# Output sums held in PSUM banks, and the first product wholly from quarters, in the tail of an attention and mixer kernel

## The chip, the cores and the metric

The kernel runs on one core of a Trainium2 chip. The metric is the device time of one execution in microseconds. Fast executions of one kernel mostly lie within 2 us of each other, and a few lie up to 5 us above, which is more than a small change is worth. So beside the times I use a second measure, from the traces alone: the time **from the V products of batch 5 to the end of the span**. The V products are four matmuls of 512 columns in the token mixing of a batch; those of batch 5 are the last landmark ahead of everything that the change touches.

The measure repeats well. The changed kernel was traced twice, the second time in a slow execution, whose granted clock was low (0.64 and 0.68) only between 10 and 30 us of the span and whose extra time lay entirely ahead of the landmark. Start of the V products in the first trace and in the second, with the spans:

```profile
221.59 0.39 PE L538 MATMUL pscore<-V_sb,ux 32*128 32x512 bf16 x2
core 0: 361.3 us, clock 1.000
```
```profile
227.38 0.39 PE L538 MATMUL pscore<-V_sb,ux 32*128 32x512 bf16 x2
core 0: 367.1 us, clock 0.981
```

361.3 - 221.59 = 139.71 us, and 367.1 - 227.38 = 139.72 us, though the spans differ by 5.8 us. Stretches of equal code agree too: the V products of the last mixing start 75.47 or 75.48 us behind the landmark in the kernel before and in experiments 2, 3 and 6, and 70.76 or 70.77 us behind it in the changed kernel, its repeat and experiments 4, 5, 8, 9 and 11. But the spans are printed to 0.1 us, so the difference of two measures is good to about 0.1 us. Where two kernels have the same end, the start of the last product, printed to 0.01 us, is the sharper mark.

## The reference, cut to what matters

```python
# attention with a decay bias, 8 batches x 8 heads x 576 tokens x 64
scores = scale * q @ k.T;  scores = where(causal, -1e9, scores + minimum(bias, 0))
x = softmax(scores) @ v                      # as (8, 576, 512)
# low-rank token mixing, then the channel mixer
u = x + (x.T @ U @ V).T
out = u + relu(u @ w_ch1) @ w_ch2            # 512 -> 2048 -> 512
```

The mixer's 4608 tokens go in NG = 9 groups of 512. Both mixer products are done by quarters: a 2 x 2 product of blocks with seven block products in place of eight, from sums of blocks, and sums of the seven results.

Of the kernel before, what the change touches and what calls it, by code (L numbers as in the profile page):

```python
# [39 lines left out]
def kernel(  # L40
# [33 lines left out]
    work = ctx.enter_context(tc.tile_pool(name="work", bufs=2))  # L74
    ps_w = ctx.enter_context(tc.tile_pool(name="ps_w", bufs=4, space=bass.MemoryType.PSUM))
    ps_s_pool = tc.tile_pool(name="ps_s", bufs=2, space=bass.MemoryType.PSUM)
# [606 lines left out]
    def outputs_by_quarters(g, hT, u_sd):  # L683
# [3 lines left out]

        def bank():
            return pwork().rearrange("p (i d) -> p i d", i=2)

        def product(acc, a, b, i):
            for kt in range(HF):
                nc.tensor.matmul(  # L693
                    acc[:, i, :],
                    lhsT=a[:, kt, ds(i * 128, 128)],
                    rhs=b[:, kt, :],
                    start=(i == 0 and kt == 0),
                    stop=(kt == HF - 1),
                    skip_group_check=True,
                )  # L700
# [22 lines left out]

        halves = range(2)
        U2 = work.tile([128, 2, HD], FP32, tag="U2", name="U2", bufs=1)
        p1 = bank()
# [43 lines left out]
        send(o22, 1, 1)  # L770
        if g == NG - 1:
            o21 = quarter()
            add_u(o21, U2, 1, 0)
            for i, lo, hi in ((0, 0, HD), (1, 0, 128), (1, 128, HD)):
                p4 = bank()
                for kt in range(HF):
                    nc.tensor.matmul(
                        p4[:, 0, lo:hi],
                        lhsT=A22[:, kt, ds(i * 128, 128)],
                        rhs=B_4[:, kt, lo:hi],  # L780
                        start=(kt == 0),
                        stop=(kt == HF - 1),
                    )
                add(o21[:, i, lo:hi], o21[:, i, lo:hi], p4[:, 0, lo:hi])
                (nc.sync if lo == 128 else nc.scalar).dma_start(
                    out=out_flat[ds(g * 512 + 256 + i * 128, 128), lo:hi], in_=o21[:, i, lo:hi]
                )
            return
        p4 = bank()
# [27 lines left out]
    def first_weight_sums():  # L817
        for dst, a, b, op in (
            (W_3, W11, W21, ALU.subtract),
            (W_1, W21, W22, ALU.add),  # L820
            (W_2, W_1, W11, ALU.subtract),
            (W_4, W12, W_2, ALU.subtract),
        ):
            placed(lambda: nc.vector.tensor_tensor(dst, a, b, op=op))
            yield

# [14 lines left out]
    def hidden_by_quarters(u, u_sums, hT, sets):  # L841
# [36 lines left out]
        def at(e, slot):  # L878
# [29 lines left out]
            elif slot == 13:  # L908
                product(p.w, W22, u_4, e, False)
                add(e, 1, 0, p.U2, p.w)  # L910
                if sets == 4 and e in (1, 2):
                    first_sums(hT, e == 1)
            return True
# [6 lines left out]

    def by_token(u):
        u_sd = work.tile([128, 4, 4, 128], BF16, tag="u_sd", name="u_sd", bufs=1)
        nc.sync.dma_start_transpose(
# [4 lines left out]
    def chanmix(g, hT=None, done=0):  # L928
        u = uT_of.pop(g)
        if g > 0:  # L930
            hT = work.tile([128, NF, 512], BF16, tag="hT", name="hT")
            sums = weight_sums() if g == 1 else iter(())
        for nf in range(done, NF):
# [7 lines left out]
            if nf == (3 if g > 0 else NF - 1):  # L941
                u_sd = by_token(u)
            yield
        if g > 0:
# [23 lines left out]

    fill = []

    pace = [0, 16]

    def step_fill():
        pace[0] += pace[1]
        if pace[0] < 16:
            return
        pace[0] -= 16
        while fill:
            if next(fill[0], fill) is not fill:
                return  # L980
            fill.pop(0)
# [146 lines left out]
    pace[1] = 11  # L1128
    made_w = first_weight_sums()
    for n in range(2 * PB, NP + 2):  # L1130
        b, hp = divmod(n, PB)
        if hp == 0 and b < B - 1:
            load(b + 1)
        if NP - 2 <= n <= NP:
            step(made_w)
        mixing = seqmix(b - 1) if hp == 1 and b > FT else iter(())
# [17 lines left out]
        if hp == 1 and FT < b < B:  # L1154
            fill.append(chanmix(b - 1))
            pace[1] = 12 if b < 4 else 12
        if 2 * PB < n <= NP:
            run(values(n - 1, pT_of(n - 1)))
        if hp == 0 and 2 <= b < B - 1:
            load_v(b + 1)  # L1160
    pace[1] = 16
    ps_s_pool.__exit__(None, None, None)
    ps_t = ctx.enter_context(tc.tile_pool(name="ps_t", bufs=4, space=bass.MemoryType.PSUM))
    tail_sums = {}
    tail_sums[NG - 2] = token_sums(
        uT(NG - 2), v_slots[1].rearrange("p a b c -> p (a b c)")
    )
    step(made_w)
    xT_again = work.tile([128, 4, 640], BF16, tag="xT", name="xT", bufs=1)
# [6 lines left out]

    for g, sets, fills in ((NG - 2, 2, range(13)), (NG - 1, 4, (1, 3, 5, 7, 9, 11, 13, 16, 19, 22, 25, 25, 26, 26))):
        u = uT_of.pop(g)
        hT = work.tile([128, NF, 512], BF16, tag="hT", name="hT")
        if g < NG - 1:  # L1180
            fill.append(hidden_plain(u, hT, (4, 12, 5, 13, 6, 14, 7, 15)))
        for at, _ in enumerate(hidden_by_quarters(u, tail_sums[g], hT, sets)):
# [9 lines left out]
        while fill:  # L1192
            step_fill()
        u_sd = by_token(u)
        fill.append(outputs_by_quarters(g, hT, u_sd))
# [33 lines left out]
```

## The kernel before: what the change and the argument touch

The second product of a group. Each of the seven products takes a fresh bank of four rotating ones. ScalarE and VectorE keep the running sum U2 in SBUF:

```python
U2 = work.tile([128, 2, HD], FP32, tag="U2", bufs=1)
p1 = bank()                                   # pwork(): one of 4 rotating banks
for i in halves: product(p1, A11, B11, i); ...; yield
nc.scalar.copy(U2, p1)
p2 = bank(); ...                              # product(p2, A12, B21)
o = quarter(); add_u(o, U2, 0, 0); add(o, o, p2); send(o, 0, 0)
p6 = bank(); ...; add(U2, U2, p6)
p5 = bank(); ...; o22 = quarter(); add(o22, U2, p5)
p3 = bank(); ...; o12 = quarter(); add_u(o12, o22, 0, 1); add(o12, o12, p3)
p7 = bank(); ...; add_u(o22, o22, 1, 1); add(U2, U2, p7); add(o22, o22, p7)
if g == NG - 1:                               # the end: p4 in three pieces
    o21 = quarter(); add_u(o21, U2, 1, 0)
    for i, lo, hi in ((0, 0, HD), (1, 0, 128), (1, 128, HD)):
        p4 = bank(); ...                      # 8 matmuls
        add(o21[:, i, lo:hi], o21[:, i, lo:hi], p4[:, 0, lo:hi]); ...dma_start(...)
```

`add_u` adds the residual from `u_sd`, the group's tokens turned by a transposing transfer (`by_token`). A `yield` ends a piece; the pieces of a group's mixer are the *fill*, which the loop over the heads runs between its own steps at a pace:

```python
def step_fill():
    pace[0] += pace[1]
    if pace[0] < 16: return
    pace[0] -= 16
    while fill: ...                           # one piece of the first generator
# tail: first product of groups 7 and 8 by quarters, the fill between
for g, sets, fills in ((NG - 2, 2, range(13)), (NG - 1, 4, (1, 3, 5, ...))):
    if g < NG - 1: fill.append(hidden_plain(u, hT, (4, 12, 5, 13, 6, 14, 7, 15)))
    for at, _ in enumerate(hidden_by_quarters(u, tail_sums[g], hT, sets)):
        for _ in range(fills.count(at)): step_fill()
    while fill: step_fill()
    u_sd = by_token(u)
    fill.append(outputs_by_quarters(g, hT, u_sd))
```

The softmax here doesn't subtract the row's maximum and nothing guards it: scores larger than these inputs give would overflow.

## Time and profile before

| | before |
|---|---|
| time, median of 4 runs | 363.95 us (363.54 to 364.96) |
| span of the trace | 362.9 us |
| PE busy, share of the span | 97% |
| V products of batch 5 to the end | 362.9 - 222.30 = 140.60 us |
| start of the last product to the end | 362.9 - 356.69 = 6.21 us |

The lines that carry the reading are in the prediction. Its method is that PE's true pace is read from the spacing of the starts in long runs. A matmul's record is longer than that: 0.273 us against a spacing of 0.109 for 256 columns. These last 0.16 us are pipeline and no work. A wait in brackets is counted from the end of the record before it, so it can be 0.16 us shorter than the hole in the starts. And "x3" in a run of four with a hole of 0.21 us behind it is a record missing from the trace, not a wait.

### The profile page before, as it was taken

How to read it: one execution, taken by the hardware profiler on the slowest of the kernel's cores; microseconds unless marked ns; L12 is line 12 of the kernel's file. 1: busy time of each engine (PE TensorE's matmuls, PEld its weight loads, DVE VectorE, ACT ScalarE, POOL GpSimd, SP SyncE). 2: the span in 40 equal slices, each digit the busy share in tenths (PEclk: the TensorE clock that was granted, in tenths of full speed). 3: DMA queues.
4: the chain of work that ended last, by engine and by line, in shares of the span. 5: the costliest groups of instructions: out<-in, count | busy, mean ns of one | idle time of the engine just before them, and what ended most of it. 6: DMA issues, size and time to landing. Idle time of an engine off the chain costs nothing.

```text
span 362.9 us, 9555 instructions
## 1 busy us (share of the span) xinstructions
PE 351.2 (97%) x3973; PEld 254.9 (70%) x4015; DVE 278.0 (77%) x607; ACT 209.5 (58%) x319; POOL 84.8 (23%) x108
## 2 busy tenths in 40 slices
PE   8899999999999999999999999999999999999995
PEld 4566566666588667876688667876688568678884
DVE  8766776779789758985699569975899279676985
ACT  3784985747762678257843786357734641565710
POOL 8988263614040404040314022000000000000000
PEclk9999999999999999999999999999999999999999
DMA  7999999999999899979994999260213400500053
GB/s 104 170 203 200 162 181 132 155 152 111 118 105 106 149 119 63 94 101 117 133 101 63 141 136 85 52 164 20 20 49 95 89 18 33 144 2 31 29 132 102
DMA packets 155107, 37.94 MB, mean 105 GB/s; under 512 B 138680, under 2 KB 153432, under 8 KB 155064
## 3 DMA queue, kind: packets, MB, share of 16 engines
q0 software_dynamic: 110016, 18.50, 78.9%
q1 hardware_dynamic: 44760, 18.64, 30.0%
q8 instruction: 31, 0.51, 0.7%
q10 hardware_dynamic: 288, 0.20, 0.2%
q14 instruction: 12, 0.10, 0.1%
HBM read 37.25 MB, written 9.70 MB: 129 GB/s over the span
## 4 chain that ended last, share of the span: by engine, by line
PE 77%; DVE 11%; ACT 6%; issue 3%; DMA 2%; SPq 0%; DVEq 0%; ACTq 0%
PE pwork L648 24%; PE pwork L693 20%; PE pscore L402 9%; PE pwork L462 7%; PE pwork L315 4%; PE parts L853 3%; PE pwork L658 3%; DVE slot L675 2%; ACT hT L936 2%; DVE o_sb L707 2%; DVE uT L516 2%; DMA slot<-hT 2%; ACT pT L417 1%; PE pscore L216 1%; PE pscore L648 1%
## 5 line engine op out<-in xcount | busy, mean ns | idle before, releaser
L648 PE MATMUL pwork<-uT,w_sb 128*128 128x512 bf16 x431 | 113.8, 379 | 2.1 <-ACT hT L936 0.5
L417 ACT ACTIVATE pT<-pscore 128x1024 bf16<-128x1024 f32 x56 | 57.2, 1030 | 55.7 <-PE pscore L402 54.8
L936 ACT ACTIVATE hT<-pwork 128x512 bf16<-128x512 f32 x108 | 65.2, 609 | 31.2 <-PE pwork L648 31.1
L648 PEld LDWEIGHTS <-w_sb 128*128 128x128 bf16 x480 | 41.2, 98 | 37.3 <-issue 0.7
L402 PE MATMUL pscore<-slot 68*128 68x320 bf16 (+1 forms) x500 | 56.0, 246 | 1.0 <-DMA slot<-hT 0.7
L402 PEld LDWEIGHTS <-slot 68*128 68x128 bf16 x564 | 41.2, 97 | 17.9 <-issue 1.3
L693 PEld LDWEIGHTS <-hT 128*128 128x128 bf16 x496 | 46.1, 98 | 7.2 <-issue 0.7
L186 POOL DMA_DIRECT2D v_slot<-in_v_dram x36 | 30.3, 857 | 80.1 <-PE pwork L462 69.1
L693 PE MATMUL pwork<-w_sb,hT 128*128 128x256 bf16 x384 | 48.2, 273 | 0.0
L347 DVE TENSOR_TENSOR pT<-pT,keep 128x512 bf16<-128x512 bf16 (+1 forms) x81 | 28.6, 353 | 20.2 <-ACT pT L417 14.0
L335 DVE COPY slot<-pwork 64x576 bf16<-64x576 bf16 x76 | 34.4, 453 | 4.7 <-PE pwork L315 3.9
L462 PEld LDWEIGHTS <-pT 128*128 128x128 bf16 x870 | 32.4, 98 | 5.6 <-issue 0.6
L462 PE MATMUL pwork<-v_slot,pT 128*128 128x65 bf16 x870 | 35.5, 193 | 0.2 <-DVE uT L516 0.2
L693 PE MATMUL pwork<-w_sum,slot 128*128 128x256 bf16 x256 | 32.0, 272 | 0.8 <-DVE o_sb L707 0.7
L472 DVE TENSOR_TENSOR x_sb<-pwork,rec 128x320 bf16<-128x320 f32 x64 | 31.2, 488 | 1.3
L428 ACT ACTIVATE pT<-pscore 128x1024 bf16<-128x1024 f32 x29 | 30.2, 1042 | 2.4 <-PE pscore L402 2.2
L338 DVE COPY slot<-pwork 64x576 bf16<-64x576 bf16 x29 | 23.3, 803 | 5.6 <-PE pwork L315 3.9
L471 DVE RECIPROCAL rec<-pwork 128x5 f32<-128x5 f32 x64 | 12.0, 189 | 20.0 <-PE pwork L462 19.5
L693 PEld LDWEIGHTS <-slot 128*128 128x128 bf16 x256 | 24.0, 98 | 4.5 <-issue 1.6
L112 POOL DMA_DIRECT2D q_sd<-in_q_dram x6 | 12.6, 2105 | 45.6 <-PE pwork L315 43.6
L707 DVE TENSOR_TENSOR o_sb<-o_sb,pwork 128x512 f32<-128x512 f32 (+2 forms) x34 | 21.8, 647 | 0.7 <-PE pwork L693 0.3
L315 PEld LDWEIGHTS <-q_sd 72*128 72x128 bf16 x256 | 15.1, 98 | 9.0 <-DMA q_sd<-in_q_dram 0.9
(159 smaller groups left out, 497.8 us busy)
## 6 DMA issues: line engine op xcount, KB each, us to landing
out_dram<-o_sb SPq DMA_DIRECT2D x35, 256.0 KB
w_sb<-in_moe_w_ch_dram POOLq DMA_DIRECT2D x4, 1024.0 KB, 12.7
v_slot<-in_v_dram POOLq DMA_DIRECT2D x28, 128.0 KB, 6.9
q_sd<-in_q_dram POOLq DMA_DIRECT2D x5, 576.0 KB, 15.1
k_sd<-in_k_dram POOLq DMA_DIRECT2D x5, 576.0 KB, 20.6
q_sd<-in_q_dram POOLq DMA_DIRECT2D x4, 288.0 KB, 12.8
k_sd<-in_k_dram POOLq DMA_DIRECT2D x4, 288.0 KB, 12.9
q_sd<-in_q_dram POOLq DMA_DIRECT2D x4, 144.0 KB, 4.9
```

The costliest lines, as they stand in the source:

```text
L186: nc.gpsimd.dma_start(out=vt[:rows_t, t, :, 0:D], in_=v[b, :, ds(t * 128, rows_t), :].rearrange("h p d -> p h d"),)
L315: nc.tensor.transpose(tps[hh][:, c, t2, :], src[:, 2 * hp + hh, ds(t2 * 128, 128)], identity[:TP, :TP],)
L335: copies(n, hh, par)(by_run[:, :, :, par, :], src)
L402: nc.tensor.matmul(dst, lhsT=slot[0:KA, hh, ds(S + j * 128, 128)], rhs=slot[0:KA, hh, lo:hi], start=True, stop=True,)
L417: nc.scalar.activation(pT[:, hh, 0:1024], near, EXP, scale=scale)
L428: nc.scalar.activation(pT[:, :, 1024:1536], mid.rearrange("p (a b) -> p a b", a=2), EXP, scale=scale)
L462: nc.tensor.matmul(po[:, i, :], lhsT=pT[:, hh, ds(place(j, i), 128)], rhs=vt[:, j, h, :], start=(j == 0), stop=(j == i), skip_group_check= ...
L472: nc.vector.tensor_tensor(x_sb[:, hp, :, ds(hh * D, D)], po[:, :, 0:D], rec.to_broadcast([128, 5, D]), op=ALU.mult,)
L648: nc.tensor.matmul(f1, lhsT=w1_sb[:, kt, ds(nf * 128, 128)], rhs=u[:, kt, :], start=(kt == 0), stop=(kt == 3),)
L693: nc.tensor.matmul(acc[:, i, :], lhsT=a[:, kt, ds(i * 128, 128)], rhs=b[:, kt, :], start=(i == 0 and kt == 0), stop=(kt == HF - 1), skip_g ...
L707: nc.vector.tensor_tensor(dst, a, b, op=ALU.add)
L936: nc.scalar.activation(hT[:, nf, :], f1, RELU)
```

## The change

Its intent: in the last three groups the running sum of the products stays in one bank (`y`), to which each product adds, so that VectorE reads it out instead of keeping U2. A second bank holds the other sum. Group 7's first product is done wholly by quarters. To have banks that nothing else rotates through, the work pool is freed after the last mixing and split into two rotating and two held ones; the fill is slowed so that group 6's output pieces come after that.

```diff
+        if g >= NG - 3:
+            y = bank("y")                       # held
+            for i in halves: product(y, A11, B11, i) ...
+            o11 = quarter(); add_u(o11, y, 0, 0)
+            x = bank("z"); ...                  # A12 B21
+            add(o11, o11, x); send(o11, 0, 0)
+            for i in halves: product(y, A_2, B_2, i, False) ...
+            o21 = quarter(); add_u(o21, y, 1, 0)
+            w = bank("z"); product(w, A_3, B_3, 0)
+            for i in halves: product(y, A_1, B_1, i, False)
+            o22 = quarter(); add_u(o22, y, 1, 1)
+            product(w, A_3, B_3, 1); add(o22, o22, w); send(o22, 1, 1)
+            if g == NG - 1: add(o21, o21, w)
+            for i in halves: product(y, A_4, B22, i, False)
+            o12 = quarter(); add_u(o12, y, 0, 1); send(o12, 0, 1)
+            ...                                 # last product: into w, or in the last group in three pieces
... (first_weight_sums: in halves, made during group 6's first product)
... (by_token: for groups 7 and 8 issued ahead of the first product, into an x_sb buffer)
+        if NG - 3 in expanded and not ps_tail:
+            return                              # step_fill: the gate
-            pace[1] = 12 if b < 4 else 12
+            pace[1] = 12 if b < 6 else 10
+    while NG - 3 not in expanded: step_fill()
+    ps_w_pool.__exit__(None, None, None)
+    ps_w = ...tile_pool(name="ps_x", bufs=2, space=PSUM)
+    ps_tail.append(...tile_pool(name="ps_q", bufs=1, space=PSUM))
-    for g, sets, fills in ((NG - 2, 2, range(13)), ...
+    for g, sets, fills in ((NG - 2, 4, (0, 0, 2, 4, 6, 8, 10, 12, 14, 17, 20, 23, 25, 26)), ...
```

More of the change, by code (lines that the diff above doesn't have):

```diff
@@ L74 @@
     work = ctx.enter_context(tc.tile_pool(name="work", bufs=2))
-    ps_w = ctx.enter_context(tc.tile_pool(name="ps_w", bufs=4, space=bass.MemoryType.PSUM))
+    ps_w_pool = tc.tile_pool(name="ps_w", bufs=4, space=bass.MemoryType.PSUM)
+    ps_w = ps_w_pool.__enter__()
+    ps_tail = []
     ps_s_pool = tc.tile_pool(name="ps_s", bufs=2, space=bass.MemoryType.PSUM)
@@ L686, in outputs_by_quarters, with bank, product @@
         A_3 = A21
-        def bank():
-            return pwork().rearrange("p (i d) -> p i d", i=2)
-        def product(acc, a, b, i):
+        def bank(tag="y"):
+            if g < NG - 3:
+                tile = pwork()
+            else:
+                tile = ps_tail[0].tile([128, 512], FP32, tag=tag, name="quarter", bufs=1)
+            return tile.rearrange("p (i d) -> p i d", i=2)
+        def product(acc, a, b, i, begin=True):
             for kt in range(HF):
@@ L696, in product @@
                     rhs=b[:, kt, :],
-                    start=(i == 0 and kt == 0),
+                    start=(begin and i == 0 and kt == 0),
                     stop=(kt == HF - 1),
@@ L724, in outputs_by_quarters @@
         halves = range(2)
+        if g >= NG - 3:
+            y = bank("y")
+            for i in halves:
+                product(y, A11, B11, i)
+                total(*((A_1, A21, A22, ALU.add), (A_2, A_1, A11, ALU.subtract))[i], 1)
+                yield
+            o11 = quarter()
+            add_u(o11, y, 0, 0)
+            x = bank("z")
+            for i in halves:
+                product(x, A12, B21, i)
+                total(A_3, A11, A21, ALU.subtract, i)
+                yield
+            add(o11, o11, x)
+            send(o11, 0, 0)
+            for i in halves:
+                product(y, A_2, B_2, i, False)
+                total(A_4, A12, A_2, ALU.subtract, i)
+                yield
+            o21 = quarter()
+            add_u(o21, y, 1, 0)
+            w = bank("z")
+            product(w, A_3, B_3, 0)
+            yield
+            for i in halves:
+                product(y, A_1, B_1, i, False)
+                yield
+            o22 = quarter()
+            add_u(o22, y, 1, 1)
+            product(w, A_3, B_3, 1)
+            yield
+            add(o22, o22, w)
+            send(o22, 1, 1)
+            if g == NG - 1:
+                add(o21, o21, w)
+            for i in halves:
+                product(y, A_4, B22, i, False)
+                yield
+            o12 = quarter()
+            add_u(o12, y, 0, 1)
+            send(o12, 0, 1)
+            if g == NG - 1:
+                for i, lo, hi in ((0, 0, HD), (1, 0, 128), (1, 128, HD)):
+                    p4 = ps_t.tile([128, 512], FP32, tag="t", name="parts").rearrange(
+                        "p (i d) -> p i d", i=2
+                    )
+                    for kt in range(HF):
+                        nc.tensor.matmul(
+                            p4[:, 0, lo:hi],
+                            lhsT=A22[:, kt, ds(i * 128, 128)],
+                            rhs=B_4[:, kt, lo:hi],
+                            start=(kt == 0),
+                            stop=(kt == HF - 1),
+                        )
+                    add(o21[:, i, lo:hi], o21[:, i, lo:hi], p4[:, 0, lo:hi])
+                    (nc.sync if lo == 128 else nc.scalar).dma_start(
+                        out=out_flat[ds(g * 512 + 256 + i * 128, 128), lo:hi],
+                        in_=o21[:, i, lo:hi],
+                    )
+                return
+            for i in halves:
+                product(w, A22, B_4, i, False)
+                yield
+            add(o21, o21, w)
+            send(o21, 1, 0)
+            yield
+            return
@@ L770, in outputs_by_quarters @@
         send(o22, 1, 1)
-        if g == NG - 1:
-            o21 = quarter()
-            add_u(o21, U2, 1, 0)
-            for i, lo, hi in ((0, 0, HD), (1, 0, 128), (1, 128, HD)):
-                p4 = bank()
-                for kt in range(HF):
-                    nc.tensor.matmul(
-                        p4[:, 0, lo:hi],
-                        lhsT=A22[:, kt, ds(i * 128, 128)],
-                        rhs=B_4[:, kt, lo:hi],
-                        start=(kt == 0),
-                        stop=(kt == HF - 1),
-                    )
-                add(o21[:, i, lo:hi], o21[:, i, lo:hi], p4[:, 0, lo:hi])
-                (nc.sync if lo == 128 else nc.scalar).dma_start(
-                    out=out_flat[ds(g * 512 + 256 + i * 128, 128), lo:hi], in_=o21[:, i, lo:hi]
-                )
-            return
         p4 = bank()
@@ L823, in first_weight_sums @@
         ):
-            placed(lambda: nc.vector.tensor_tensor(dst, a, b, op=op))
-            yield
+            for k in range(2):
+                placed(
+                    lambda: nc.vector.tensor_tensor(dst[:, k, :], a[:, k, :], b[:, k, :], op=op)
+                )
+                yield
     def u_quarters(u):
@@ L910, in at @@
                 add(e, 1, 0, p.U2, p.w)
-                if sets == 4 and e in (1, 2):
-                    first_sums(hT, e == 1)
+                if sets == 4 and e in (2, 3):
+                    first_sums(hT, e == 2)
             return True
@@ L919, in hidden_by_quarters, with by_token @@
                     yield
-    def by_token(u):
-        u_sd = work.tile([128, 4, 4, 128], BF16, tag="u_sd", name="u_sd", bufs=1)
+    def by_token(u, late=False):
+        if late:
+            x_sb = work.tile([128, PB, 5, 128], BF16, tag="x_sb", name="x_sb")
+            u_sd = x_sb.rearrange("p a b c -> p (a b c)")[:, 0:2048].rearrange(
+                "p (a b c) -> p a b c", a=4, b=4
+            )
+        else:
+            u_sd = work.tile([128, 4, 4, 128], BF16, tag="u_sd", name="u_sd", bufs=1)
         nc.sync.dma_start_transpose(
@@ L931, in chanmix @@
             hT = work.tile([128, NF, 512], BF16, tag="hT", name="hT")
-            sums = weight_sums() if g == 1 else iter(())
+            sums = {1: weight_sums, NG - 3: first_weight_sums}.get(g, lambda: iter(()))()
         for nf in range(done, NF):
@@ L942, in chanmix @@
                 u_sd = by_token(u)
+            if nf == NF - 1:
+                expanded.append(g)
             yield
@@ L969 @@
     fill = []
+    expanded = []
     pace = [0, 16]
@@ L977, in step_fill @@
         pace[0] -= 16
+        if NG - 3 in expanded and not ps_tail:
+            return
         while fill:
@@ L1128 @@
     pace[1] = 11
-    made_w = first_weight_sums()
     for n in range(2 * PB, NP + 2):
@@ L1133 @@
             load(b + 1)
-        if NP - 2 <= n <= NP:
-            step(made_w)
         mixing = seqmix(b - 1) if hp == 1 and b > FT else iter(())
@@ L1161 @@
     pace[1] = 16
+    while NG - 3 not in expanded:
+        step_fill()
     ps_s_pool.__exit__(None, None, None)
+    ps_w_pool.__exit__(None, None, None)
+    ps_w = ctx.enter_context(tc.tile_pool(name="ps_x", bufs=2, space=bass.MemoryType.PSUM))
+    ps_tail.append(ctx.enter_context(tc.tile_pool(name="ps_q", bufs=1, space=bass.MemoryType.PSUM)))
     ps_t = ctx.enter_context(tc.tile_pool(name="ps_t", bufs=4, space=bass.MemoryType.PSUM))
@@ L1167 @@
     )
-    step(made_w)
     xT_again = work.tile([128, 4, 640], BF16, tag="xT", name="xT", bufs=1)
@@ L1175, in hidden_plain @@
             yield
-    for g, sets, fills in ((NG - 2, 2, range(13)), (NG - 1, 4, (1, 3, 5, 7, 9, 11, 13, 16, 19, 22, 25, 25, 26, 26))):
+    for g, sets, fills in ((NG - 2, 4, (0, 0, 2, 4, 6, 8, 10, 12, 14, 17, 20, 23, 25, 26)), (NG - 1, 4, (1, 3, 5, 7, 9, 11, 13, 16, 19, 22, 25, 25, 26, 26))):
         u = uT_of.pop(g)
+        u_sd = by_token(u, True)
         hT = work.tile([128, NF, 512], BF16, tag="hT", name="hT")
-        if g < NG - 1:
-            fill.append(hidden_plain(u, hT, (4, 12, 5, 13, 6, 14, 7, 15)))
         for at, _ in enumerate(hidden_by_quarters(u, tail_sums[g], hT, sets)):
@@ L1193 @@
             step_fill()
-        u_sd = by_token(u)
         fill.append(outputs_by_quarters(g, hT, u_sd))
```

## The prediction

> **What bounds the kernel now.** I read the page first (busy shares, the chain that ended last), then the table by stage, then the timeline of each engine over the last 65 us, where the change acts.
>
> ```profile
> PE 351.2 (97%) x3973; PEld 254.9 (70%) x4015; DVE 278.0 (77%) x607; ACT 209.5 (58%) x319; POOL 84.8 (23%) x108
> ...
> PE 77%; DVE 11%; ACT 6%; issue 3%; DMA 2%; SPq 0%; DVEq 0%; ACTq 0%
> ```
>
> The matrix engine is busy in 97% of the span and carries 77% of the chain. The table by stage, of which I take four stretches (length, then busy us and count of PE, PEld, DVE, ACT), says that this holds in the tail too:
>
> ```profile
> 300.00:310.00 10.00, 9.92 (x95) 8.75 (x93) 10.00 (x22) 2.27 (x4) 0.00 (x0) 1.00 0.16 55
> 310.00:320.00 10.00, 9.89 (x64) 6.26 (x65) 5.37 (x10) 6.42 (x12) 0.00 (x0) 1.00 0.43 105
> 320.00:330.00 10.00, 10.00 (x90) 8.58 (x89) 9.01 (x15) 5.30 (x10) 0.00 (x0) 1.00 0.01 2
> 330.00:340.00 10.00, 9.76 (x89) 8.44 (x87) 6.55 (x11) 6.44 (x12) 0.00 (x0) 1.00 0.08 28
> ```
>
> PE idles 0.43 us in these 40 us, although VectorE is full in the first stretch and at 90% in the third. Busy is not peak, so I take the spacing of long runs from the chain of waits in order of time (start, us, what):
>
> ```profile
> 280.79 7.12 PE pwork L648 x33
> ...
> 346.29 10.58 PE pwork L693 x96
> ```
>
> A product of 512 columns costs 7.12/33 = 0.216 us, one of 256 costs 10.58/96 = 0.110 us (0.109 in runs of 8, 0.87/8). Both runs are gap-free. So in the tail only three things are worth anything: fewer matmul columns, a wait of PE removed, or a shorter stretch behind the last matmul. That stretch, from the timeline:
>
> ```profile
> 356.69 1.93 PE L777 MATMUL pwork<-w_sum,hT 128*128 128x256 bf16 x24
> 356.89 0.69 DVE L707 TENSOR_TENSOR U<-U,pwork 128x512 f32<-128x512 f32 x1 [0.76 <-PE pwork L693]
> 357.49 0.68 DVE L707 TENSOR_TENSOR o_sb<-o_sb,pwork 128x512 f32<-128x512 f32 x1
> 358.09 0.68 DVE L707 TENSOR_TENSOR o_sb<-U,u_sd 128x512 f32<-128x512 f32 x1
> 358.88 0.82 DVE L707 TENSOR_TENSOR o_sb<-o_sb,pwork 128x256 f32<-128x256 f32 x3
> ...
> 359.72 0.35 SPq L785 DMA_DIRECT2D out_dram<-o_sb  x1
> ```
>
> The first p4 product (8 matmuls) is done about 357.6, but VectorE still has three adds of the previous product, so it reaches p4 only at 358.88 and ends at 359.70. The last transfer then takes 3.2 us to the end of the span at 362.9. All matmuls are over by 358.62: VectorE alone holds back the end.
>
> **What the Trainium skill says.** "VectorE: DVE Perf Modes", section "The perf-mode tier table": a tensor_tensor with fp32 or PSUM operands runs at 1x, with bf16 in SBUF at 2x. The trace agrees: 512 fp32 elements per partition take 0.68 us, 1024 bf16 elements 0.69 us. So an add that moves from an SBUF sum to the bank itself costs the same; only the number of adds counts. "PSUM — Partial Sum Buffer", section "The four PSUM rules": a matmul without the first flag adds where the bank has been written, and a synchronised read amid a group is allowed. This is what the held banks rest on; the first product of the trace of before already does it (tile `parts`, where a later product adds to y after a copy). "Perfetto Trace Analysis", section "Optimization Strategy": the same gap repeating can mean that too few buffers exist; relevant since the work banks in the tail go from 4 to 2 plus 2 held ones. The trace of before has no such repeated gap.
>
> **The change part by part.**
>
> (a) First product of group NG-2. Before, 2 of its 4 sets are quarters and 8 row blocks are plain: 8 x 4 = 32 matmuls of 512 columns. After, two more sets: 2 x 7 x 4 = 56 of 256. 32 x 0.216 = 6.91, 56 x 0.109 = 6.10: **-0.8 us** of PE, all on the path. ScalarE and VectorE get instead of 8 ReLUs (0.60 each) three copies and three ReLU instructions a set on ScalarE (about 3.5 us a set) and three adds a set (0.6 us back to back); both have room: the last group has that load today, with one PE wait of 0.24 us at 330.68.
>
> (b) Sums in held banks, three groups. Adds of an output group (leaving out the sums of weights or hidden values) fall from 11 to 7 (8 in the last group), and a ScalarE copy of 0.57 goes. That is 11 adds x 0.6 = 6.6 us of VectorE and 1.7 of ScalarE. The matmuls stay the same in number. As PE is the bound, this is hidden work: **0**, but for the end.
>
> (c) The end. Call Y the start of the last product. Before, VectorE's last add ends at Y + 3.0 (356.69 to 359.70). After, VectorE has a single add of 0.68 left at Y (starts Y + 0.2, done Y + 0.9), then follows PE: the last 8 narrow matmuls end at Y + 1.95, a 128-column add of about 0.2 follows: Y + 2.15. **-0.85 us**; the 3.2 us of transfer stay.
>
> (d) New dependency in the last group, which nothing interleaves: y must be read by an add before the next product may write it. The time between is one half product, 8 x 0.109 = 0.87 us; the add starts 0.2 us after the last matmul was issued and takes 0.69 us. Twice about 0.05: **+0.1 us**.
>
> (e) The fill runs slower (10 of 16, not 12) from the sixth batch on and must not enter the output stage of group NG-3 before the banks are freed. The instruction order shows what follows: the last mixing, and the one before it, are now filled by hidden products, 12 matmuls of 512 in three banks behind the four V products, where before it was output products, two parts to a bank. With four rotating banks the third of these must wait for VectorE to empty a bank of the mixing. Before, that stretch reads:
>
> ```profile
> 297.77 0.39 PE L536 MATMUL pwork<-V_sb,ux 32*128 32x512 bf16 x2
> 298.09 1.05 PE L693 MATMUL pwork<-w_sb,hT 128*128 128x256 bf16 x8
> 298.98 3.02 PE L693 MATMUL pwork<-w_sum,slot 128*128 128x256 bf16 x24
> 301.84 0.28 PE L561 MATMUL pwork<-V_end,ux 128*128 128x64 bf16 x4
> ```
>
> After, in the last mixing VectorE first owes two sums (1.3 us, ending some 0.7 us after the V products), then 1.2 us for the pair, 0.7 for the third bank: free at about 2.6 us, wanted at 2 x 0.86 = 1.7 us: **+0.8 us**. In the mixing before, with no hidden sums ahead of it, it is free at about 2.2: **+0.4**, and the last small product waits for the fourth bank, behind a sum: about +0.2; the wait of 0.49 on a ReLU that stands there now probably remains.
>
> (f) Waits that should go: the 0.24 at 330.68 and the output waits on VectorE in the sixth batch (0.41 at 228.61), as the fill shifts; perhaps half: **-0.3**. Splitting the weight sums and moving the token-major transposes earlier changes no PE work; both are off the path.
>
> Sum: -0.8 - 0.85 + 0.1 + 0.8 + 0.6 - 0.3 = **-0.45 us**. My bank waits in (e) assume the worst order of VectorE; I halve them, to +0.7, which gives about -1.1 us, so 362.4 us.
>
> **Rivals.** One: relieving VectorE is worth much more, as it is 10.00 of 10.00 busy at 300 to 310 and on 11% of the chain. For: the chain shows runs of VectorE between 295 and 301 and 320 and 329. Against: PE had no gap there (9.92 and 10.00), so those links run beside it; the time could not go below 361 without cutting matmuls. Two: the bank waits eat all of it. Two held banks leave two work banks, and hidden products in the place of output products make the mixing wait on VectorE in two places, up to 1.4 us, plus new waits in the interleaved groups, where y is used by every product: that would make 363.5 to 364.5. For it: the longest PE waits of before (0.41, 0.49) are of exactly this kind. Against: in the interleaved part, 2 to 3 hidden pieces of 0.44 us lie between the use of y and its next write. Three: slower filling makes the attention part wait on ScalarE, as there is less to fill; its exponentials take about 3.4 us a pair of heads of 8 us, so I think not; 0 to +1 us.
>
> **Range and chances.** Certain: -0.8 in matmuls. Nearly so: -0.85 at the end. Unsure: -0.7 to +1.4 in waits. That gives 361.4 to 363.3, widened by the spread of 0.8 us of the three runs of before: 361.2 to 363.8. A change of 2% is 7.3 us; no sum here comes near it either way.
>
> **What would show it.** (a) Products of 512 columns fall by 32 and those of the first product by quarters rise by 56. (c) VectorE's last add ends about 0.25 us after the last matmul, and the stretch from the last matmul's start to the span's end shrinks by 0.85. (d) In the last group two PE waits under 0.15 us on VectorE. (e) PE waits on VectorE's emptying just behind the V products of the last two mixings, together 0.5 to 1.4 us. Rival one would show as more than 2 us less PE idle before the last group; rival two as PE waits of over 2 us in sum from 250 us on. It would be wrong, above all, if the attention part from the sixth batch on takes longer or shorter by itself than the sum of its matmuls says.

## The result, and the profile after

The changed kernel takes 362.97 us (median of 4 runs, 362.67 to 363.03), the kernel before 363.95 us in the same rounds. The ratio is 0.9967, with a 95% interval of 0.9944 to 0.9991. A ratio here is the mean time of one kernel's fast runs over that of the other's of the same rounds, so it is not quite the ratio of the medians. By the traces, the changed part takes 139.71 us in place of 140.60: **-0.89 us**. The spans differ by 1.6 us, but 0.71 us of that (222.30 against 221.59) lies ahead of anything that was changed.

The same stretches of the table by stage as in the prediction. PE now has no idle time that the table shows, and VectorE has room:

```profile
300.00:310.00 10.00, 10.00 (x95) 8.97 (x92) 7.89 (x16) 5.90 (x10) 0.00 (x0) 1.00 0.28 68
310.00:320.00 10.00, 10.00 (x94) 8.94 (x92) 8.26 (x13) 7.11 (x12) 0.00 (x0) 1.00 0.16 54
320.00:330.00 10.00, 10.00 (x95) 8.95 (x93) 6.89 (x12) 5.92 (x10) 0.00 (x0) 1.00 0.14 47
330.00:340.00 10.00, 10.00 (x93) 8.81 (x91) 5.76 (x9) 6.56 (x11) 0.00 (x0) 1.00 0.03 8
```

**The columns.** Weight loads lack fewer records than matmuls, and one stands before each matmul. Groups of PE's loads, before and after (the line of the plain first product, then the lines of that by quarters):

```profile
L648 PEld LDWEIGHTS <-w_sb 128*128 128x128 bf16 x480 | 41.2, 98 | 37.3 <-issue 0.7 <-DVE x_sb L472 0.5 <-DVE slot L338 0.3
L853 PEld LDWEIGHTS <-w_sb 128*128 128x128 bf16 x72 | 7.0, 98 | 2.2 <-issue 0.6
L853 PEld LDWEIGHTS <-slot 128*128 128x128 bf16 x72 | 7.0, 98 | 1.5
L853 PEld LDWEIGHTS <-v_slot 128*128 128x128 bf16 x24 | 2.3, 98 | 0.5
```
```profile
L650 PEld LDWEIGHTS <-w_sb 128*128 128x128 bf16 x448 | 38.3, 98 | 35.9 <-issue 1.3 <-DVE x_sb L474 0.5 <-DVE slot L340 0.3
L911 PEld LDWEIGHTS <-slot 128*128 128x128 bf16 x96 | 9.4, 98 | 1.1
L911 PEld LDWEIGHTS <-w_sb 128*128 128x128 bf16 x96 | 9.3, 98 | 1.2 <-issue 0.2
L911 PEld LDWEIGHTS <-v_slot 128*128 128x128 bf16 x32 | 3.1, 98 | 0.4
```

480 to 448 is 32 fewer of the plain kind, 168 to 224 is 56 more by quarters, as the diff says.

**The end.** The timeline of the changed kernel behind the start of the last product:

```profile
356.06 1.93 PE L778 MATMUL parts<-w_sum,hT 128*128 128x256 bf16 x24
356.26 0.69 DVE L713 TENSOR_TENSOR o_sb<-quarter,x_sb 128x512 f32<-128x512 f32 x1 [0.53 <-PE quarter L699]
357.14 0.73 DVE L713 TENSOR_TENSOR o_sb<-o_sb,parts 128x256 f32<-128x256 f32 x2 [0.18 <-PE parts L778]
...
358.03 0.29 DVE L713 TENSOR_TENSOR o_sb<-o_sb,parts 128x128 f32<-128x128 f32 x1 [0.16 <-PE parts L778]
358.35 0.35 SPq L786 DMA_DIRECT2D out_dram<-o_sb  x1
```

VectorE now waits for PE before each add, where before it came from one add to the next; its last add starts 1.97 us after the last product began, not about 2.7. 361.3 - 356.06 = 5.24 us to the end, in place of 6.21: -0.97 us. VectorE's last add ends 2.26 us after that start (358.03 + 0.29 - 356.06) in place of 3.01, which is 0.75 of it. The other 0.22 lies behind the add, in the last transfer: 3.0 us to the end of the span, not 3.2. Why that is shorter was not looked into.

**The waits.** Waits of PE from 240 us on, before and after:

```profile
PE pwork L648 <- ACT hT L936: 0.5, 1, 0.5
PE parts L853 <- ACT hT L907: 0.2, 1, 0.2
```
```profile
PE pwork L650 <- ACT hT L1000: 0.9, 1, 0.9
PE quarter L699 <- DVE uT L518: 0.3, 1, 0.3
```

This view leaves out short waits, which the spacing of the starts shows. First one place in the kernel before, in the first product of the last group, then the places in the changed kernel's timeline:

```profile
329.84 0.60 PE L853 MATMUL parts<-xT,w_sb 128*128 128x256 bf16 x4
330.68 0.60 PE L853 MATMUL parts<-uT,w_sb 128*128 128x256 bf16 x4 [0.24 <-ACT hT L907]
```

```profile
256.88 2.75 PE L650 MATMUL pwork<-uT,w_sb 128*128 128x512 bf16 x12 [0.92 <-ACT hT L1000]
...
292.69 2.76 PE L650 MATMUL pwork<-uT,w_sb 128*128 128x512 bf16 x12
295.56 0.29 PE L563 MATMUL pwork<-V_end,ux 128*128 128x64 bf16 x4
295.69 0.60 PE L911 MATMUL parts<-uT,w_sb 128*128 128x256 bf16 x4
296.56 1.92 PE L699 MATMUL quarter<-w_sb,hT 128*128 128x256 bf16 x16 [0.27 <-DVE uT L518]
...
350.55 1.04 PE L699 MATMUL quarter<-w_sb,hT 128*128 128x256 bf16 x8
351.63 1.91 PE L699 MATMUL quarter<-w_sum,slot 128*128 128x256 bf16 x16
353.38 1.04 PE L699 MATMUL quarter<-w_sb,hT 128*128 128x256 bf16 x8
354.32 1.91 PE L699 MATMUL quarter<-w_sb,v_slot 128*128 128x256 bf16 x16
```

Read from the starts, with each matmul of 512 columns at 0.216 us and of 256 at 0.109:

- The first matmul behind the V products of batch 6, at 256.88 in the stretch of batch 7: the wait is 0.92 in place of 0.49 (in the kernel before it stands at 260.48), 0.43 more.
- The twelve matmuls at 292.69, in the last mixing, take 2.87 us to the next start, where 12 x 0.216 = 2.59: 0.28 of waiting ahead of the mixing's last small product, at 295.56. It takes a bank that VectorE has emptied only by then.
- The four at 295.69 take 0.87 to the next start, where 4 x 0.109 = 0.44: 0.43 of waiting ahead of the first held product.
- The half product at 350.55 takes 1.08 to the next start, where 8 x 0.109 = 0.87: 0.21. At 353.38 it is 0.94: 0.07.

That is 1.42 us of new waiting. Two waits of the kernel before are gone. From 329.84 to 330.68 it took 0.84 for 0.44 of work: 0.40. And its last mixing waited for a bank too: the 24 matmuls at 298.98, which the prediction shows, take 2.86 us to the next start, where 24 x 0.109 = 2.62: 0.24. There PE waits for a bank that an output add of VectorE reads, from 300.24 to 300.92. So the waits grew by about 0.8 us. The start of the last product says how much it is in all: 356.69 - 222.30 = 134.39 us behind the landmark before, 356.06 - 221.59 = 134.47 after. That is 0.08 later, with 0.80 us fewer columns, so 0.88 of waiting; what the list does not hold of it is in gaps under 0.15 us. With the columns and the end, -0.80 - 0.97 + 0.88 = -0.89. So the change earned 1.8 us and gave back about half.

### The profile page after: what moved, and what is told of

Its sections match the earlier page's. It is cut to its first block, busy times and chain, and to the rows that moved or that the text cites. A ratio compares the mean times of both kernels' runs of the same rounds, so it can differ in the third digit from the quotient of the medians.

```text
span 361.3 us, 9653 instructions
## 1 busy us (share of the span) xinstructions
PE 353.0 (98%) x4039; PEld 257.1 (71%) x4039; DVE 276.4 (77%) x604; ACT 213.2 (59%) x322; POOL 84.8 (23%) x108
## 4 chain that ended last, share of the span: by engine, by line
PE 77%; DVE 11%; ACT 5%; DMA 4%; issue 2%; SPq 0%; DVEq 0%; ACTq 0%
PE pwork L650 22%; PE pwork L699 12%; PE pscore L404 9%; PE quarter L699 9%; PE pwork L464 7%; PE parts L911 6%; PE pwork L317 4%; PE pwork L660 3%; DMA xT<-x_sb 2%; DVE slot L677 2%; DVE uT L518 2%; ACT hT L1000 2%; DVE o_sb L713 2%; DMA slot<-hT 1%; ACT pT L419 1%
## 5 line engine op out<-in xcount | busy, mean ns | idle before, releaser
L650 PE MATMUL pwork<-uT,w_sb 128*128 128x512 bf16 x432 | 108.0, 379 | 1.1 <-ACT hT L1000 0.9
L650 PEld LDWEIGHTS <-w_sb 128*128 128x128 bf16 x448 | 38.3, 98 | 35.9 <-issue 1.3
L404 PE MATMUL pscore<-slot 68*128 68x320 bf16 (+1 forms) x500 | 55.2, 246 | 0.3
L699 PE MATMUL pwork<-w_sb,hT 128*128 128x256 bf16 x240 | 30.6, 273 | 0.0
L699 PE MATMUL pwork<-w_sum,slot 128*128 128x256 bf16 x160 | 20.3, 272 | 0.7 <-DVE o_sb L713 0.7
L699 PE MATMUL quarter<-w_sb,hT 128*128 128x256 bf16 x144 | 18.0, 273 | 0.3 <-DVE uT L518 0.3
```

What stands on the lines that cost most here:

```text
L404: nc.tensor.matmul(dst, lhsT=slot[0:KA, hh, ds(S + j * 128, 128)], rhs=slot[0:KA, hh, lo:hi], start=True, stop=True,)
L650: nc.tensor.matmul(f1, lhsT=w1_sb[:, kt, ds(nf * 128, 128)], rhs=u[:, kt, :], start=(kt == 0), stop=(kt == 3),)
L699: nc.tensor.matmul(acc[:, i, :], lhsT=a[:, kt, ds(i * 128, 128)], rhs=b[:, kt, :], start=(begin and i == 0 and kt == 0), stop=(kt == HF - ...
```

## The experiments

Each is a small edit of the changed kernel or of the kernel before. The measure is the time from the V products of batch 5 to the end (before 140.60, changed 139.71). All outputs were correct. The full times mostly cannot tell the kernels apart, and are given where they say something. Experiments 3, 7, 8, 9 and 11 were executed once, so their state is unknown by their times; the granted clock in their traces is 1.000. Waits are given as the views print them, unless the starts are named.

**1. The changed kernel once more** (no edit).

> The changed kernel once more, for a narrower interval and to stand beside the three others on one chip. Sum theory (0.8 us fewer matmul columns, about 0.95 us less behind the last product, about 0.8 us more waits of PE): 0.9 to 1.2 us less than before, ratio 0.9968. Rival (relief of VectorE frees more than that): ratio under 0.995.

Ratio 0.9970 (0.9928 to 1.0012), 139.72 us. Its trace is the slow one. The ratio again lies where the sum has it.

**2. The held end alone**, in the kernel before:

```diff
+        if g == NG - 1:
+            ...  # the changed kernel's output sums, y, x and w from the four work banks
```

> The kernel before with one part of the change alone: the last group's output sums held in banks, taken from the four work banks; pools, pace, group 7's first product and the other groups stay. Sum theory: the time from the start of the last product to the end of the span falls from 6.2 to about 5.25 us, PE waits of about 0.25 us appear on the held bank; time -0.7 us. Rival (the gain comes from the relief in all three groups): next to nothing, within 0.2 us of before.

It lost: 141.63 us, 1.03 more than before (ratio 1.0009, 0.9974 to 1.0043). The end itself did what was expected. The first add out of the held bank did not. Timeline of VectorE and of the transfer queue, with PE's next product:

```profile
346.58 1.97 SPq L990 DMA_TRANSPOSE u_sd<-uT  x1
```
```profile
351.18 0.69 DVE L707 TENSOR_TENSOR o_sb<-pwork,u_sd 128x512 f32<-128x512 f32 x1 [0.69 <-DMA u_sd<-uT]
```
```profile
351.93 1.91 PE L693 MATMUL pwork<-w_sum,slot 128*128 128x256 bf16 x16 [1.57 <-DVE o_sb L707]
```

The add needs the transposed tokens, which land only about 351 us. In the kernel before nothing waited for that add: U2 was in SBUF and the bank free. With the sum held in the bank, PE may not add the next product until the add has read it, and waits 1.57 us. So the earlier transposes, which the prediction called off the path, are part of what makes the held bank pay. Neither theory had this; experiment 3 tests it.

**3. The same with the transpose early**:

```diff
+        if g == NG - 1:
+            u_sd = by_token(u, True)          # ahead of the first product
```

> As end_alone, with the last group's token-major transpose issued ahead of its first product, as the changed kernel does. Theory (end_alone lost 1.6 us because the first add out of the held bank waited for that transpose): the wait falls to about 0.25 us in all, and from the V products of batch 5 to the end it takes about 139.9 us in place of 141.63 (before 140.60, changed 139.71). Rival (the held bank itself costs that wait): stays at 141 or more.

140.02 us: the wait of 1.57 is gone, and 1.61 us with it. The start of the last product to the end takes 361.7 - 356.36 = 5.34 us. The part alone is worth 0.58 us against before, its 0.9 us at the end less some 0.3 on the held bank.

**4. Group 7's first product as before**, in the changed kernel:

```diff
-((NG - 2, 4, (0, 0, 2, 4, 6, ...)), ...
+((NG - 2, 2, (0, *range(13))), ...
+        if g < NG - 1: fill.append(hidden_plain(u, hT, (4, 12, 5, 13, 6, 14, 7, 15)))
```

> The changed kernel with group 7's first product again half from quarters, half plain (32 matmuls of 512 columns in place of 56 of 256). Sum theory: 0.8 us longer than the changed kernel, all in matmul columns, so about as fast as before less 0.3 us. Rival (the extra copies and adds on ScalarE and VectorE cost what the columns save): no difference to the changed kernel.

140.60 us: 0.89 more than the changed kernel by the printed spans. By the start of the last product it is 0.83 (356.70 - 221.40 = 135.30 us behind the landmark, against 134.47), and 0.8 of that are the columns. The extra copies and adds cost PE nothing. Ratio to before 0.9984 (0.9951 to 1.0017).

**5. The last group's outputs as before**, in the changed kernel:

```diff
-        if g >= NG - 3:
+        if NG - 1 > g >= NG - 3:              # the last group: separate banks, U2 in SBUF
+        ...                                   # its old end, p4 in three pieces, put back
```

> The changed kernel with the last group's outputs as before (separate banks, sums kept in SBUF by VectorE and ScalarE). Sum theory: the stretch from the start of the last product to the end is 6.2 us again and the waits of about 0.3 us on the held bank go, so 0.6 to 0.7 us longer than the changed kernel. Rival: no difference, if the relief in the other two groups lets VectorE catch up by itself.

140.56 us: 0.85 more than the changed kernel, 6.25 us from the start of the last product to the end. Relief in the other two groups does not shorten the end by itself.

**6. Both gains without the rest**: the kernel of experiment 3 with group 7's first product by quarters (and its transpose early too); pace, pools and the sums of groups 6 and 7 as before.

```diff
-((NG - 2, 2, range(13)), ...
+((NG - 2, 4, (0, 1, 2, 3, 5, 7, 9, 12, 15, 18, 21, 24, 26)), ...
-            fill.append(hidden_plain(...))
```

> As end_early, with group 7's first product wholly from quarters too; fill pace, banks and the output sums of groups 6 and 7 stay as before. Sum theory: columns -0.85, end -0.95, waits of about +0.25 and none of the changed kernel's waits behind the V products: 139.0 to 139.3 us from the V products of batch 5 to the end, 0.4 to 0.7 us less than the changed kernel. Rival (the held banks in groups 6 and 7 are needed, as VectorE and ScalarE have no room for two more sets beside the old output sums): PE waits of 0.5 us and more on VectorE or ScalarE between 300 and 325 us, and 139.7 or more.

144.05 us, and the one clear loss in full time: 367.83 us, ratio 1.0091 (1.0051 to 1.0132). Waits of PE from 240 us on:

```profile
PE parts L920 <- ACT hT L974: 1.5, 1, 1.5
PE parts L920 <- DVE hT L933: 1.2, 2, 0.6
PE parts L920 <- ACT pT L970: 1.1, 2, 0.7
PE pwork L648 <- ACT hT L1009: 0.5, 1, 0.5
```

They lie between 312 and 324 us. The rival expected waits there, but for want of VectorE and ScalarE. The timeline shows another cause: from 311 us on PE has only parts of the first product, with no output piece between. At the pace of before, eight of group 6's fourteen output pieces have been spent before the first part (64 weight loads, 8 a piece), and the other six, the last at 310.17, do not last for four sets. Each part then waits for a copy, an add or a ReLU of an earlier part. Experiment 11 bears this out: there the old sums of groups 6 and 7 stand beside four sets as well, but all fourteen pieces last, and PE waits little.

**7. The old pace**, in the changed kernel:

```diff
-            pace[1] = 12 if b < 6 else 10
+            pace[1] = 12
```

> The changed kernel with the fill's pace of before (12 of 16) to the end. Theory (the pace was lowered only so that the fill lasts until the banks are freed): group 6's hidden rows run out before the last mixing is over, the gate then leaves PE nothing to fill with, and PE waits of 2 to 5 us in sum appear around the last mixing; time to the end 142 to 144 us. Rival (the lowered pace is harmless or harmful by itself, it causes the 0.92 us wait on ScalarE in batch 7): that wait goes back to 0.49, and the time falls.

141.83 us, 2.1 more. Waits of PE from 240 us on:

```profile
PE parts L911 <- DVE uT L518: 1.6, 1, 1.6
PE quarter L699 <- DVE uT L518: 1.0, 1, 1.0
PE pwork L650 <- ACT hT L1000: 0.5, 1, 0.5
PE pscore L538 <- DVE ux L508: 0.4, 1, 0.4
```

Group 6's hidden rows ran out before the last mixing was over, and nothing filled its dependent steps. The wait in batch 7 went back from 0.92 to 0.49 us: the slower fill causes 0.43 of it, so both expectations hold in part. The lower pace costs 0.4 and saves 2.5.

**8. The two new pools in the other order**, so that `y` lies on another bank:

```diff
-    ps_w = ...name="ps_x"...
-    ps_tail.append(...name="ps_q"...)
+    ps_tail.append(...name="ps_q"...)
+    ps_w = ...name="ps_x"...
```

> The changed kernel with the order of the two new pools exchanged, so that the first held bank lies on another of the freed banks. Theory (the wait of 0.27 us before the first held product is for the very bank that the mixing's last small sum is read from): it goes, 139.3 to 139.5 us in place of 139.71. Rival (a freed pool is waited for as a whole): unchanged, 139.7.

139.72 us, no difference; the wait stands at 0.26. The particular bank is not the cause. The rival is left: the freed pool is waited for as a whole, or both of its halves are.

**9. Held sums in the last group alone**, in the changed kernel; the four rotating banks stay, so no gate:

```diff
-        if g >= NG - 3:
+        if g == NG - 1:
-        if NG - 3 in expanded and not ps_tail: return
-    (the pools ps_x and ps_q; y, x and w come from ps_w)
```

> The changed kernel with the held sums in the last group alone: groups 6 and 7 keep separate banks and the old adds, from four rotating work banks; pace 10, early transposes and the whole first product from quarters stay. Sum theory (held sums of groups 6 and 7 are worth nothing, PE does the same work): 139.4 to 139.9 us from the V products of batch 5 to the end (changed kernel 139.71), with the 0.27 us wait at the freed bank gone. Rival (with two more sets, VectorE has no room for the 8 more adds, 4.8 us): PE waits of 0.5 us and more on VectorE or ScalarE between 300 and 345 us, 140.5 or more.

140.75 us, 1.04 more, just as the rival expected. But the order of pieces had moved too: without the gate two output pieces were spent behind the last mixing (at 295.71 and 296.71), and at the end of group 7's first product two were missing, so that six parts follow each other. The waits stand there:

```profile
318.67 0.60 PE L907 MATMUL parts<-v_slot,w_sb 128*128 128x256 bf16 x4
319.10 0.60 PE L907 MATMUL parts<-v_slot,slot 128*128 128x256 bf16 x4
320.43 0.60 PE L907 MATMUL parts<-uT,slot 128*128 128x256 bf16 x4 [0.73 <-ACT pT L957]
321.34 0.60 PE L907 MATMUL parts<-v_slot,w_sb 128*128 128x256 bf16 x4 [0.31 <-DVE hT L920]
```

**10. The three new waits mended**, in the changed kernel:

```diff
-            nc.scalar.activation(hT[:, nf, :], f1, RELU)
+            if (g, nf) == (NG - 4, 10): nc.vector.tensor_scalar_max(hT[:, nf, :], f1, 0.0)
+            else: nc.scalar.activation(hT[:, nf, :], f1, RELU)
-            if g > 0 and nf in (12, 14): first_sums(...)
+            if 0 < g < NG - 3 and nf in (12, 14): first_sums(...)
+    (group 6's first sums, forced behind group 7's token sums in VectorE's order)
+    (last group: the two sums A_4 forced behind the add that reads y for o21)
```

> The changed kernel with its three new waits mended: one hidden row's ReLU of batch 7's mixing on VectorE instead of ScalarE (wait of 0.92 us), group 6's first sums after the last mixing's emptying instead of ahead of it (0.28 and 0.27 us), the last group's fourth sum after the add that frees the held bank (0.2 us). If each wait has the cause I give, they all but go: 138.2 to 138.7 us in place of 139.71, 0.3% less time than the changed kernel. Where a wait stays in its place, its cause was another.

139.32 us. The end went as meant: the wait of 0.21 fell to 0.07. In the last mixing the 0.28 went, but PE only came sooner to the first held product and waited 0.46 there in place of 0.27. In batch 7 the ReLU on VectorE cut 0.92 to 0.59, which then ended with the next exponential in ScalarE's queue. Ratio to before 0.9961 (0.9918 to 1.0004); in full time it cannot be told from the changed kernel.

**11. As 9, with the gate kept**, so that PE's pieces come in the changed kernel's order:

```diff
+        if NG - 3 in expanded and not ps_tail: return
+    ps_tail.append(True)                      # after the last mixing; no pool is changed
```

> As undo_held67, but with the changed kernel's gate, so that no output piece of group 6 is spent behind the last mixing and PE's order is piece by piece that of the changed kernel. Undo_held67 lost 1.04 us in two waits at 319 to 321 us, where three parts follow each other with no piece between. Theory (a piece was missing there, and the held sums of groups 6 and 7 are themselves worth nothing): the two waits go, 139.4 to 139.75 us (changed kernel 139.71). Rival (VectorE and ScalarE have no room for the old sums beside two more sets): they stay or move, 140.3 or more.

139.90 us: 0.85 of the 1.04 us were the two missing pieces. The held sums of groups 6 and 7, with the change of pools that they need, are worth 0.19 us by the printed spans and 0.14 by the start of the last product (356.41 - 221.80 = 134.61, against 134.47). Neither expectation was met to the letter. The wait of 0.27 at the freed pool (0.43 by the starts) is gone, as there is none. Instead gaps of 0.29 and 0.19 us appear behind the runs of eight matmuls at 311.69 and 319.41: PE waits for a ReLU of ScalarE, then for an add of VectorE, on which the old sums lie as well (21.10 us busy between 300 and 325, in place of 19.61). Waits over 240 us are down to one line:

```profile
PE pwork L649 <- ACT hT L996: 0.9, 1, 0.9
```

**12. As 11, with the mends of 10.**

> As held67_gate with the three mends of the run mended. If the wait of 0.46 us at the first held product came from the change of pools, it has no place here, and with the old sums harmless this is the shortest: 138.8 to 139.0 us from the V products of batch 5 (mended 139.32). If VectorE is short of room, 139.5 or more.

139.27 us, the shortest of all, though not apart from experiment 10 (139.32), and 362.20 us in time, ratio 0.9953 (0.9929 to 0.9977): faster than before beyond the interval. It is 0.44 us shorter than the changed kernel by the traces, without any of the pool changes. The wait at the freed pool is gone, but three gaps of 0.19, 0.32 and 0.17 us by the starts, at 300.5, 306.1 and 319.3 us, took part of it. The first two end with ScalarE and the third with VectorE. So the 138.8 to 139.0 expected was not reached.

## Why the prediction was right

The time (362.4 predicted, 362.97 measured, in rounds where before was 0.4 slower than known) and the size of the change (-1.1 predicted, -0.89 by the traces) were right. The two gains and their causes were understood. That the waits came near the forecast is largely luck: +1.4 was halved by judgement, and none of the three bank waits stood where it was put. Step by step:

- **(a) columns, -0.8:** right. The loads count 32 and 56; undoing the part costs 0.83 us.
- **(b) sums in held banks, 0 but for the end:** right in size. Groups 6 and 7 gain 0.14 to 0.19 us from it (experiment 11). The first rival, that relief of VectorE is worth more by itself, is refuted.
- **(c) the end, -0.85:** right in size; 0.97 in the trace, and 0.85 when undone. VectorE's part is 0.75, not 0.85, and 0.22 came from the last transfer, which was to stay at 3.2 us.
- **(d) the held bank in the last group, +0.1:** too small. It is 0.28. The second add came as reckoned (0.07 of waiting), the first later: VectorE had a sum in hand when the bank was ready (0.21), and went when that sum was moved.
- **(e) the last two mixings, +1.4 at worst and +0.7 after halving:** the size is about 0.9 (0.43 + 0.04 + 0.43), the account of it mostly wrong. In batch 7 the +0.4 and +0.2 did not come: the twelve matmuls there take 2.59 us to the next start, without a wait. PE waited ahead of them for a ReLU on ScalarE, behind an exponential of 1.05 us, not for VectorE's emptying; that wait was expected to stay at 0.49 and grew to 0.92. In the last mixing the third bank, +0.8, cost nothing: its first matmul starts at 294.42, with no hole before it. VectorE's two sums do stand ahead of its emptying, as said, but what they delay is the last small product: 0.28, and it goes when they are moved (experiment 10). Only 0.04 of it is new: the lines that the prediction shows of the kernel before have a bank wait of 0.24 in them (24 matmuls in 2.86 us), which it did not read. Then PE waited again at the freed pool, 0.43, which the prediction did not see.
- **(f) waits that go, -0.3:** 0.40 by the starts went at 330.68 (0.24 in the view); the one of 0.41 in the sixth batch stayed, as it lies ahead of the first slowed step.
- **"Splitting the weight sums and moving the token-major transposes earlier ... both are off the path":** wrong for the transposes. With a held bank, their late landing is worth 1.6 us (experiments 2 and 3). The prediction priced the change as a whole, in which they are early, so this did not touch the sum.
- **The second rival**, that the bank waits eat all, has the right stretch and the wrong size: 0.9 us net of 1.8.
- **The third rival**, that slower filling makes the attention wait on ScalarE, is 0.43 us of truth, and pays for itself: without it 2.1 us are lost.
- **The range** is mis-summed at its lower end: 363.56 - 0.8 - 0.85 - 0.7 is 361.2, not 361.4. The result lies far from it.

What stays open is whether the wait at the first held product is for the whole freed pool. Experiment 8 excludes the one bank and experiment 11 shows that it goes with the pool change; a kernel that frees the pool with all of its banks read long before was not run. Experiment 11 also takes the held sums away with the pools, so the two are not parted. Open too is why the last transfer is 0.22 us shorter.

## What to carry to other kernels

Where one engine is the bound, as PE here, an edit's gain is its instructions on that engine, the stretch behind its last instruction, and its waits; relief of VectorE showed here only where its backlog stood at the end. Take the waits from the spacing of the starts, in the kernel before as well: a wait that was there already is not the change's. A sum held in a bank turns the reader of the bank into a gate for the next product, so everything that the reader needs, a transfer above all, must be there first. Work that fills gaps is a stock: count its pieces through the whole schedule, as moving two pieces cost 0.85 us here and a pace that spends the stock too soon 2 to 4.

## What the Trainium skill lacked or had wrong

- "PSUM — Partial Sum Buffer", section "The four PSUM rules", says that a partial sum may be read, synchronised, in the middle of a group. The runs agree (all outputs correct), but the page does not say what the read costs the matmul stream: from a half product's start to the held bank's next matmul 1.08 and 0.94 us passed where the half product takes 0.87, and PE waited 1.57 us when the reader lacked its other operand.
- "Perfetto Trace Analysis", section "Optimization Strategy", links repeated gaps to too few buffers. No page has the case seen here, of a single wait: after a pool was freed and split, the first use waited 0.27 us with the same number of banks, in both orders of the new pools, and 0 in the run without held sums in groups 6 and 7 and without the change of pools.
- "Perfetto Trace Analysis", section "Identifying the Most-Contended Engine", warns that matmul busy time misleads, and names weight-load busy time as a good metric, beside the share of peak arithmetic. Here it depends on the width of the matmuls: a load takes 98 ns, so at full pace it is busy 45% of the time with 512 columns (0.098 of 0.216 us) and 90% with 256 (0.098 of 0.109), both worked out from the traces. In the tail before it read 6.26 of 10 us between 310 and 320 and 8.58 between 320 and 330, though PE issued as steadily in the first as in the second. The spacing of starts in long runs was what found every wait.
- "TensorE: Matmul & The Clock Gate", section "Back-to-back issue gap", gives some 131 ns as the sustained spacing of matmuls of 512 columns and 216 ns as the isolated one. In this kernel's long runs of loads and matmuls it was 216 ns (33 in 7.12 us): the isolated figure, not the sustained one. The same page's account of the clock gate has this spacing for back-to-back matmuls as well, so the page contradicts itself and the trace sides with the longer figure.
